# Two-stage fused kernel on one core: the head mix runs two places behind its premix, with six exponent tiles and a 2 KB ring for GpSimd's transfers

## The chip, the cores and the metric

The kernel runs on one core of a Trainium2 chip. A core has a matrix engine (TensorE; PE in the profile, its weight loads PEld), a vector engine (DVE), an activation engine (ACT), GpSimd (POOL) and a queue that only issues transfers (SP). Each engine takes its own instructions strictly in the order in which the program wrote them, and waits on semaphores where it needs the result of another. The metric is the device time of one execution in microseconds; lower is better. The kernel before takes 1709.07 us, the median of three runs (1707.4 to 1711.44).

## The reference

The inputs are q, k and v of 8 batches, 12 heads, 448 tokens and 64 channels, two 12x12 matrices that mix heads, and two weights of a feed-forward layer of width 2048. All is float32.

```python
def _attn_ref(q, k, v, w_pre, w_post):
    scale = 1.0 / np.sqrt(q.shape[-1])
    scores = scale * np.matmul(q, k.transpose(0, 1, 3, 2))
    scores = np.einsum('bhij,hg->bgij', scores, w_pre)
    scores = scores - np.max(scores, axis=-1, keepdims=True)
    attn = np.exp(scores)
    attn = attn / (np.sum(attn, axis=-1, keepdims=True) + 1e-09)
    attn = np.einsum('bhij,hg->bgij', attn, w_post)
    return np.matmul(attn, v)

def _moe_ref(x, w_in, w_out):      # x: 3584 tokens of 768 channels
    h = x @ w_in
    g = h - np.tanh(h)
    return g @ w_out
```

So the attention mixes the heads twice: once before the softmax (w_pre, "premix") and once after it (w_post, "mix").

## The kernel before, in words

The program has an attention part (until about 855 us) and a feed-forward part after it. The change touches the attention part, and through one number the transfers that GpSimd issues in the feed-forward part.

**Blocks and groups.** A block is 120 query tokens of one batch (the fourth of a batch has 88). For each block `scores` (L874) multiplies q and k head by head into PSUM, and ACT and DVE copy the result into the tile `s`, whose rows are tokens (L879). A premix needs the 12 heads of a token on the partitions, so SP gathers 10 tokens x 12 heads = 120 rows of `s` into a tile `t` (`gather`, L907). Such a set of rows is a group; there are 45 groups in a batch and 360 in all. There are six `t` tiles, used in turn.

**Places.** The loop from L1256 on runs over places. Place `p` handles the groups 2p and 2p+1, so there are 180 places (`NPL`), and a few more to run out. At a place the program writes, in this order:

- the copy of the last mix's PSUM into the tile `at` (ACT, L967 or L974), which the loop keeps in the variable `mixed` from the place before;
- a step of `conv`, which turns the feed-forward weights into split parts on ACT, DVE and GpSimd (lines 81 to 131), its transfers being issued by SP (L766);
- the gathers for place p+2;
- `premix(p)`: 4 matmuls with `wpre` into two PSUM tiles `ps_p` (L918). There are only these two, so the next premix needs both exponents of this place done;
- `norm(p-1)`: DVE adds 1e-9 to the row sums `zs` of place p-1 and inverts them (L938, L939), GpSimd multiplies them into the mixing matrix, giving `wr` (L940);
- `expo(p)`: for each of the two PSUM tiles DVE takes the row maximum `mx` (L927) and ACT the exponent `e` with the row sum (L929). There are four `e` tiles, two for each of two places;
- what the planner has put at this place: `scores`, `values`, and the transposes of q (`prep_q`, L840) and of k (`prep_k`, L814);
- `mix(p-1)`: 16 matmuls with `e` as weights and `wr` as the moving side into `ps_o` (L957). There is one `ps_o`, so a mix also needs the `at` copy of the one before.

A matmul on float32 stands as two in the trace, so that a premix has 8 there and a mix 32.

**Values and the planner.** `values(i, t)` multiplies `at` of block i with v for half of the heads (L999). The planner (a list `halved` of jobs with a first and a last place) spreads `scores` and `values` over the places. A values job of block i may begin two places after place (f1-1)//2, in which the last group of the block stands, and is due a place after the place in which the second next block begins. The v tiles `vr` of a batch are loaded by three transfers (from L766's queue; three tiles, so that a load must wait for the values jobs that read the batch before).

**SP's order.** SP issues the gathers, the loads of q, k and v and the transfers of `conv`, all in the order of the places. If one of them waits, those behind it wait too.

**Tail.** At place 180 the loop splits the first token tiles for the feed-forward part, with five casts on ACT (L279), and mixes place 179; block 0 of the feed-forward part (L291 to L294) follows.

In the feed-forward part GpSimd issues 72 transfers of `ga`, `gb` and `gs` tiles (L647, L669, L670), 8 of `go` and 48 stores of the result (L519). The constructor of the program sets aside 4096 bytes per partition for the ring in which GpSimd writes the descriptors of its transfers.

Of the kernel before, what the change touches and what calls it, by code (L numbers as in the profile page):

```python
# [10 lines left out]
F32 = mybir.dt.float32  # L11
# [139 lines left out]
def kernel_body(  # L151
# [11 lines left out]
    nc = tc.nc  # L163
    B, H, S, D = q.shape
    P = 128
# [570 lines left out]
    with ExitStack() as st:  # L736
# [8 lines left out]
        gp = st.enter_context(tc.tile_pool(name="gp", bufs=4, side="right"))  # L745
# [175 lines left out]
        def expo(p, pss):  # L921
            zs = gp.tile([P, 3, 2], F32, name="zs", tag="zs")
            es = []
            for r, ps in enumerate(pss):

                mx = gp.tile([P, 1], F32, name="mx", tag="mx")
                nc.vector.tensor_reduce(out=mx, in_=ps, axis=AX.X, op=ALU.max, negate=True)  # L927
                e = gp.tile([P, S], F32, name="e", tag="e", bufs=4)
                nc.scalar.activation(e, ps, AF.Exp, bias=mx, scale=1.0, accum_out=zs[:, 0, r : r + 1])  # L929
                es.append(e)  # L930
            te[p] = [es, zs]
# [149 lines left out]
        for w in range(2):  # L1081
            for at in AT[w]:
                x = repeat[:, w, at : at + HP].rearrange("p (i h) -> p i h", i=GH)
# [52 lines left out]
        NG = len(groups)  # L1136
# [4 lines left out]
        NPL = NG // 2  # L1141
# [12 lines left out]
        for i in range(len(blocks)):  # L1154

            f0, f1, f2 = first[i : i + 3]
            if i + 1 < len(blocks):
                lo = max(0, (f0 - 1) // 2 - 1)
                hi = f1 // 2 - 3
                for x in range(0 if i else 1, 3):  # L1160
                    e = lo + 2 * x if lo + 4 <= hi else lo + (hi - lo) * x // 2
                    halved.append((e if i else x - 1, hi, "s", i + 1, x))
            for x in range(2):
                halved.append(((f1 - 1) // 2 + 2, f2 // 2 + 1 if f2 < NG else NPL + 7, "v", i, x))
        at_s, p, kind = {}, 0, None
        window = {i: (lo, hi) for lo, hi, k, i, _ in sorted(halved, reverse=True) if k == "s"}
        while halved:
# [84 lines left out]
            NPL - 1: [partial(load_w0, 1)],  # L1252
            NPL + 1: [block0.step],
        }
        mixed = None
        for p in range(NPL + 3):  # L1256
            if mixed:
                mixed()
                mixed = None
            if 5 <= p < NPL + 1:  # L1260
                conv.place()
            place[0] += 1
            for t in (2 * p + 4, 2 * p + 5):
                if t < NG:
                    gather(t)
            issue(6)
            if p == NPL + 1:
                for f in start.pop(p):
                    f()
            if p < NPL:  # L1270
                ps = premix(p)
            if 1 <= p < NPL + 1:
                norm(p - 1)
            if p == NPL:
                for f in x0[1:]:
                    f()
            if p < NPL:
                expo(p, ps)
            if p == NPL + 2:
                next(xq)  # L1280
                next(xq)
            for f, *a in todo[p]:
                f(*a)
            for f in sooner:
                f()
            sooner.clear()
            if 1 <= p < NPL + 1:
                mixed = mix(p - 1)
            for f in then + last:
                f()  # L1290
            then.clear()
            last.clear()
            if p == NPL - 3:
                conv.rest(now)
                early.close()
                open_early()
            if p == NPL - 1:
                early_ps.close()
                open_ps_h()
            for f in start.get(p, ()):  # L1300
                f()
            for _ in range(pieces.get(p, 0)):
                next(xl)
# [91 lines left out]
```

## Time and profile before

| | |
|---|---|
| median of three runs | 1709.07 us (1707.4 to 1711.44) |
| profiled execution, its own time | 1717.03 us |
| span of its profile, first to last instruction | 1715.3 us |
| granted TensorE clock, mean | 0.990 |
| PE busy | 1666.7 us (97%) |
| DVE, ACT, POOL busy | 1233.9 us (72%), 1091.9 us (64%), 586.7 us (34%) |
| premix, mix: busy on PE | 183.1 us, 316.9 us |

The profiled execution is 8.0 us longer than the median of the plain runs. Rows of the profile are read like this: a group of instructions has its line, engine, operation and tiles, the number of instructions, busy time and the mean length of one, and behind the bar the idle time of its engine just before them with what ended it. A row of the table of waits has the waiting engine and tile, who ended the wait, the sum in us, the number of waits and the longest. A row of the timeline has start, length, engine, line and tiles, and in brackets the idle time before it.

### The profile page before, as it was taken

What the parts mean: (1) busy time and instruction counts of PE and PEld (TensorE: products, weight loads), DVE (VectorE), ACT (ScalarE), POOL (GpSimd) and SP (SyncE); (2) the same over time, 40 slices, a digit from 0 to 9 for tenths busy, and PEclk for the clock granted to TensorE, in tenths of its full rate; (3) what the DMA queues carried; (4) which work ended last, traced back from release to release, by engine and by line L of the source; (5) the groups of instructions that cost most, each with busy time, mean ns of one, the idle gap of its engine ahead of it and who ended that gap; (6) DMA issues with size and microseconds to landing.
All of it is one profiled execution on the core that took longest, in us unless ns stands there. A gap on an engine that the chain in (4) does not pass through costs nothing.

```text
span 1715.3 us, 41215 instructions
## 1 busy us (share of the span) xinstructions
PE 1666.7 (97%) x16068; PEld 1385.2 (81%) x16068; DVE 1233.9 (72%) x2119; ACT 1091.9 (64%) x1920; POOL 586.7 (34%) x798
## 2 busy tenths in 40 slices
PE   8999999999999999999999999999999999999999
PEld 6777677777777677677787888888888888889999
DVE  5777767868767677775478899858888868778432
ACT  5776777767667677776577677565667455665331
POOL 1566667767657666663100011101001101101100
PEclk9999999999999999999999999999999999999999
DMA  8779879887878878866579799988999989988993
GB/s 184 217 228 257 255 232 277 250 255 247 242 236 247 256 229 260 263 190 210 193 255 339 259 325 311 342 306 322 318 341 354 368 267 339 317 311 326 400 414 136
DMA packets 322290, 475.09 MB, mean 277 GB/s; under 512 B 105264, under 2 KB 255280, under 8 KB 322096
## 3 DMA queue, kind: packets, MB, share of 16 engines
q1 hardware_dynamic: 305660, 414.34, 74.7%
q0 software_dynamic: 16128, 57.68, 8.7%
q8 instruction: 128, 2.10, 0.5%
q14 instruction: 66, 0.54, 0.1%
q10 hardware_dynamic: 308, 0.43, 0.1%
HBM read 274.73 MB, written 120.59 MB: 230 GB/s over the span
## 4 chain that ended last, share of the span: by engine, by line
PE 70%; DMA 10%; DVE 7%; ACT 5%; issue 4%; POOL 3%; SPq 1%; ACTq 0%; POOLq 0%; DVEq 0%
PE ps_o L957 11%; PE ps_h L291 7%; PE ps_h L292 7%; PE ps_h L294 7%; PE ps_m L999 6%; PE ps_p L918 6%; PE y L534 6%; PE y L532 5%; PE y L533 5%; PE ps_q L874 4%; DMA t<-s 3%; DMA gl<-gs 2%; ACT e L929 2%; DMA vr<-in_v_dram 1%; DMA w<-wo 1%
## 5 line engine op out<-in xcount | busy, mean ns | idle before, releaser
L957 PEld LDWEIGHTS ps_o<-wr,e 60*112 60x112 f32 (+1 forms) x5760 | 306.0, 176 | 45.5 <-POOL wr L940 31.3
L957 PE MATMUL ps_o<-wr,e 60*112 60x60 f32 (+1 forms) x5760 | 316.9, 260 | 15.8 <-POOL wr L940 14.5
L929 ACT ACTIVATE e<-ps_p,mx 128x448 f32<-128x448 f32 x360 | 225.1, 632 | 119.1 <-DVE mx L927 88.4
L927 DVE TENSOR_REDUCE mx<-ps_p 128x1 f32<-128x448 f32 x360 | 206.7, 616 | 112.8 <-PE ps_p L918 112.3
L967 ACT COPY at<-ps_o 112x960 f32<-112x960 f32 x156 | 154.5, 990 | 110.6 <-PE ps_o L957 110.2
L918 PE MATMUL ps_p<-t,wpre 60*64 60x448 f32 (+1 forms) x1440 | 183.1, 572 | 8.5 <-DMA t<-s 7.1
L999 PEld LDWEIGHTS ps_m<-at,vr 112*64 112x64 f32 x3072 | 149.8, 138 | 25.7 <-ACT at L974 7.5
L999 PE MATMUL ps_m<-at,vr 112*64 112x120 f32 (+1 forms) x3072 | 164.1, 264 | 3.2 <-DMA vr<-in_v_dram 2.9
L532 PE MATMUL y<-w,gh 128*128 128x384 f32 x448 | 151.2, 337 | 3.6 <-DMA w<-wo 2.2
L940 POOL TENSOR_TENSOR wr<-wpost,zs 128x120 f32<-128x120 f32 x180 | 70.1, 390 | 243.0 <-DVE zs L939 198.4
L533 PE MATMUL y<-w,gh 128*128 128x384 f32 x448 | 150.3, 336 | 0.0
L534 PE MATMUL y<-w,gl 128*128 128x384 f32 x424 | 143.3, 338 | 2.6 <-DVE gl L450 2.5
L874 PEld LDWEIGHTS ps_q<-kk,qh 64*120 64x120 f32 (+1 forms) x768 | 59.5, 175 | 82.9 <-issue 45.8
L874 PE MATMUL ps_q<-kk,qh 64*120 64x448 f32 (+1 forms) x768 | 122.6, 396 | 1.2 <-DVE kk L826 0.5
L879 DVE COPY s<-ps_q 120x448 f32<-120x448 f32 (+1 forms) x192 | 112.4, 615 | 8.3 <-PE ps_q L874 8.1
L669 POOL DMA_DIRECT2D gs<-gb x24 | 17.3, 720 | 295.4 <-DVE gb L668 295.4
L307 ACT ACTIVATE u<-h 128x1024 f32<-128x1024 f32 x56 | 59.5, 1063 | 75.0 <-DVE h L716 70.8
L879 ACT COPY s<-ps_q 120x448 f32<-120x448 f32 (+1 forms) x192 | 95.1, 539 | 7.0 <-PE ps_q L874 6.7
L647 POOL DMA_DIRECT2D gs<-ga x24 | 17.2, 719 | 229.5 <-DVE ga L330 229.5
L532 PEld LDWEIGHTS y<-w,gh 128*128 128x128 f32 x448 | 84.2, 188 | 8.8 <-issue 2.8
L533 PEld LDWEIGHTS y<-w,gh 128*128 128x128 f32 x448 | 84.1, 188 | 3.4
L534 PEld LDWEIGHTS y<-w,gl 128*128 128x128 f32 x424 | 79.5, 188 | 4.2 <-DVE gl L450 4.2
(372 smaller groups left out, 3974.1 us busy)
## 6 DMA issues: line engine op xcount, KB each, us to landing
t<-s SPq DMA_DIRECT2D x342, 210.0 KB
wa<-ss SPq DMA_DIRECT2D x96, 384.0 KB
w<-wo SPq DMA_DIRECT2D x43, 768.0 KB
gl<-gs SPq DMA_DIRECT2D x62, 512.0 KB
wa<-wi SPq DMA_DIRECT2D x72, 384.0 KB
w<-ts SPq DMA_DIRECT2D x35, 768.0 KB
gs<-gs POOLq DMA_DIRECT2D x24, 768.0 KB, 9.0
cr<-in_moe_w_in_dram SPq DMA_DIRECT2D x48, 256.0 KB
```

The costliest lines, as they stand in the source:

```text
L291: nc.tensor.matmul(ph, w[:, c, 0], xh, start=start and c == 0, stop=False, skip_group_check=True)
L532: nc.tensor.matmul(y, gh[:, tok], wh, start=first, stop=False, skip_group_check=True)
L533: nc.tensor.matmul(y, gh[:, tok], wl, start=False, stop=False, skip_group_check=True)
L534: nc.tensor.matmul(y, gl[:, tok], wh, start=False, stop=last, skip_group_check=True)
L874: nc.tensor.matmul(ps[:n, :S], qx[a, hp, :], kx[a, hp % 2], start=(x == 0), stop=(x == 2))
L879: eng(sts[i][:n, 2 * hp + j, :], ps[:n, :S])
L918: nc.tensor.matmul(pss[r][halves[j], :], wpre[k, :], ts[j][k, :], start=True, stop=True)
L927: nc.vector.tensor_reduce(out=mx, in_=ps, axis=AX.X, op=ALU.max, negate=True)
L929: nc.scalar.activation(e, ps, AF.Exp, bias=mx, scale=1.0, accum_out=zs[:, 0, r : r + 1])
L957: nc.tensor.matmul(ps[:CP, j, c * GP : (c + 1) * GP].rearrange("p (h i) -> p h i", i=GI)[:, :, r * GH : (r + 1) * GH], e[k, c * CP : (c + ...
L967: nc.scalar.copy(ats[i0][:, :, :, at : at + 2 * GI].rearrange("p c h (j i) -> p j (c h) i", j=2), ps[:CP, :, : NC * GP].rearrange("p j (x ...
L999: nc.tensor.matmul(pv[j * D : (j + 1) * D, r, :n], vt[:, j, c, :], ats[i][:, c, 2 * hp + j, :n], start=(c == 0), stop=(c == NC - 1),)
```

## The change

The loop keeps the mix one place longer: at place p it now writes `mix(p-2)` where it wrote `mix(p-1)`. `norm(p-1)` stays where it was, so `wr` of a mix is written one place ahead of it. At place 180 the mixes of places 178 and 179 both stand, with the `at` copy of 178 between them. For this the `e` tiles become six, and the ring of GpSimd's transfers shrinks from 4096 to 2048 bytes per partition; the two additional `e` tiles take 3584 bytes. The values jobs begin and are due a place later.

```diff
-                e = gp.tile([P, S], F32, name="e", tag="e", bufs=4)
+                e = gp.tile([P, S], F32, name="e", tag="e", bufs=6)
...
-                halved.append(((f1 - 1) // 2 + 2, f2 // 2 + 1 if f2 < NG else NPL + 7, "v", i, x))
+                halved.append(((f1 - 1) // 2 + 3, f2 // 2 + 2, "v", i, x) if f2 < NG else ((f1 - 1) // 2 + (3 if f1 < NG else 2), NPL + 7, "v", i, x))
...
-        mixed = None
+        mixed = []
         for p in range(NPL + 3):
-            if mixed:
-                mixed()
-                mixed = None
+            for f in mixed:
+                f()
+            mixed.clear()
...
-            if 1 <= p < NPL + 1:
-                mixed = mix(p - 1)
+            if 2 <= p < NPL + 1:
+                mixed.append(mix(p - 2))
+            if p == NPL:
+                mixed.pop()()
+                mixed.append(mix(p - 1))
...
-    nc = _bacc.Bacc("TRN2", target_bir_lowering=False, num_devices=1, dynamic_dma_scratch_size=4096)
+    nc = _bacc.Bacc("TRN2", target_bir_lowering=False, num_devices=1, dynamic_dma_scratch_size=2048)
```

What this moves, at three places of the program. First TensorE at places 0 to 3; a row has the line, what is written and read, the size and the number. Before:

```order
L918 MATMUL ps_p<-t,wpre 64x448 x4
L874 MATMUL ps_q<-kk,qh 120x448 x4
L874 MATMUL ps_q<-kk,ql 120x448 x2
L957 MATMUL ps_o<-wr,e 112x12x5 x16
L918 MATMUL ps_p<-t,wpre 64x448 x4
L874 MATMUL ps_q<-kk,qh 120x448 x4
L874 MATMUL ps_q<-kk,ql 120x448 x2
L957 MATMUL ps_o<-wr,e 112x12x5 x16
```

These rows begin with the premix of place 1, and the first mix stands behind the scores of that place. With the change, from the same premix on:

```order
L918 MATMUL ps_p<-t,wpre 64x448 x4
L874 MATMUL ps_q<-kk,qh 120x448 x4
L874 MATMUL ps_q<-kk,ql 120x448 x2
L918 MATMUL ps_p<-t,wpre 64x448 x4
L874 MATMUL ps_q<-kk,qh 120x448 x4
L874 MATMUL ps_q<-kk,ql 120x448 x2
L957 MATMUL ps_o<-wr,e 112x12x5 x16
```

Place 1 has no mix any more, and from there on each mix stands one premix and one set of scores later; GpSimd's order has not changed anywhere.

Second, SP around the three loads of v of the second batch, with what each transfer waits for (DMAHW: an earlier transfer; PE, DVE, Pool: an engine). Before:

```order
L766 DMA vr<-in_v_dram 112x4x256 [waits DMAHW3_49]
L766 DMA xs_57<-x 768x1x208 [waits DMAHW4_49,DVE_49]
L766 DMA cr<-in_moe_w_in_dram 128x2x256 [waits DMAHW5_49,Pool_49]
L766 DMA cr<-in_moe_w_in_dram 128x2x256 [waits DMAHW6_49]
L907 DMA t<-s 120x1x448 [waits DMAHW7_49,PE_49]
L907 DMA t<-s 120x1x448 [waits DMAHW0_49]
L766 DMA qr<-in_q_dram 88x12x64 [waits DMAHW1_49]
L766 DMA vr<-in_v_dram 112x4x256 [waits DMAHW2_49]
```

None of the loads of v waited for an engine here. With the change:

```order
L766 DMA vr<-in_v_dram 112x4x256 [waits DMAHW3_49,PE_49]
L766 DMA cr<-in_moe_w_in_dram 128x2x256 [waits DMAHW4_49,Pool_49]
L766 DMA cr<-in_moe_w_in_dram 128x2x256 [waits DMAHW5_49]
L907 DMA t<-s 120x1x448 [waits DMAHW6_49,PE_49]
L907 DMA t<-s 120x1x448 [waits DMAHW7_49]
L766 DMA qr<-in_q_dram 88x12x64 [waits DMAHW0_49]
L766 DMA vr<-in_v_dram 112x4x256 [waits DMAHW1_49,PE_49]
L766 DMA wi_66<-co 512x1x256 [waits DMAHW2_49,Pool_49]
L907 DMA t<-s 120x1x448 [waits DMAHW3_49]
```

The loads now carry a wait for TensorE, since the values jobs that read the old v tiles stand two places later; the same holds for the third of these loads and for the batches with index 3, 5 and 7. In the batches 2, 4 and 6 only the second load waits for TensorE, and it did so before.

Third, ACT at the tail, places 178 to 180. Before:

```order
L279 CAST xh<-xl 128x512
L967 COPY at<-ps_o 112x2x48x10
L929 ACTIVATE e,zs<-ps_p,mx 128x448 x2
L967 COPY at<-ps_o 112x2x48x10
L279 CAST xh<-xl 128x512 x5
L974 COPY at<-ps_o 112x48x9 x2
```

The five casts stood ahead of the last `at` copy, which no mix waits for. With the change:

```order
L279 CAST xh<-xl 128x512
L967 COPY at<-ps_o 112x2x48x10
L929 ACTIVATE e,zs<-ps_p,mx 128x448 x2
L967 COPY at<-ps_o 112x2x48x10
L279 CAST xh<-xl 128x512 x5
L967 COPY at<-ps_o 112x2x48x10
L974 COPY at<-ps_o 112x48x9 x2
```

One more `at` copy, that of place 178, now stands behind the casts, and the mix of place 179 needs it.

## The prediction

> **What bounds the kernel now.** I read the windows first. Columns: time, then busy us of PE, PEld, DVE, ACT and POOL with their instructions, granted clock, DMA share, GB/s.
>
> ```profile
> 25.00:855.00 830.00, 803.86 (x11629) 615.68 (x11630) 595.49 (x1506) 582.90 (x1335) 495.48 (x641) 0.98 0.79 238
> 855.00:1715.30 860.30, 842.65 (x4296) 753.34 (x4296) 627.18 (x589) 499.17 (x567) 84.41 (x130) 1.00 0.88 317
> ```
>
> TensorE sets the pace in both parts; in the attention part it is idle for 830.0 - 803.9 = 26.1 us. The table of waits says what ends its idle time there (sum, number, longest):
>
> ```profile
> PEld ps_o L957 <- POOL wr L940: 31.3, 43, 2.1
> PE ps_o L957 <- POOL wr L940: 14.5, 17, 1.7
> PE ps_p L918 <- DMA t<-s: 7.1, 6, 1.8
> PE ps_m L999 <- DMA vr<-in_v_dram: 2.9, 2, 1.9
> ```
>
> So the largest wait is the one of the mix for `wr`, in 43 of 180 places at its weight load, and in 17 long enough to be seen at the matmul. Next I looked at such places in the timeline. In this one POOL is late:
>
> ```profile
> 727.34 0.37 PE L874 MATMUL ps_q<-kk,ql 64*120 64x448 f32 x2
> 727.72 0.62 ACT L929 ACTIVATE e<-ps_p,mx 128x448 f32<-128x448 f32 x1
> 728.73 0.55 POOL L940 TENSOR_TENSOR wr<-wpost,zs 128x120 f32<-128x120 f32 x1
> 729.33 1.78 PE L957 MATMUL ps_o<-wr,e 60*112 60x60 f32 x32 [1.62 <-POOL wr L940]
> ```
>
> The scores end at 727.71, `wr` comes behind other work of POOL, and TensorE stands for 1.62 us; the exponent of this place has long ended, at 728.34. In the next one DVE is late, and everything with it:
>
> ```profile
> 100.39 0.98 PE L918 MATMUL ps_p<-t,wpre 60*64 60x448 f32 x8
> 101.81 0.37 PE L874 MATMUL ps_q<-kk,ql 64*120 64x448 f32 x2
> 102.41 0.43 DVE L94 TENSOR_SCALAR co<-cr 128x512 int32<-128x512 int32 x1
> 103.08 1.14 DVE L927 TENSOR_REDUCE mx<-ps_p 128x1 f32<-128x448 f32 x2
> 103.75 1.78 PE L957 MATMUL ps_o<-wr,e 60*112 60x60 f32 x32 [1.57 <-POOL wr L940]
> 104.40 0.62 ACT L929 ACTIVATE e<-ps_p,mx 128x448 f32<-128x448 f32 x1
> 105.46 0.98 PE L918 MATMUL ps_p<-t,wpre 60*64 60x448 f32 x8
> ```
>
> DVE works for `conv` (L94), so both the row sums that `wr` needs and the maxima that this place's exponents need come late. The next premix needs the second exponent, which ends at 105.02.
>
> **The change, term by term**, against the profiled execution (span 1715.3, own time 1717.0 us).
>
> *The wait for `wr`.* The mix of place p-2 needs a `wr` that was due one place earlier, so this wait goes. What it costs now lies between 14.5 us (idle at the matmuls) and 31.3 us (idle at the weight loads). A weight load that waits lets the matmul before it run out first:
>
> ```profile
> L957 PE MATMUL ps_o<-wr,e 60*112 60x60 f32 (+1 forms) x5760 | 316.9, 260 | 15.8 <-POOL wr L940 14.5
> ```
>
> With 0.26 us for one matmul, 31.3 - 43 x 0.26 = 20.1. I take -20.
>
> *The pace of a mix behind a wait.* A mix that had waited takes 105.46 - 103.75 = 1.71 us from its start to the premix; one that had not:
>
> ```profile
> 401.46 1.70 PE L957 MATMUL ps_o<-wr,e 60*112 60x60 f32 x32
> 403.09 0.98 PE L918 MATMUL ps_p<-t,wpre 60*64 60x448 f32 x8
> ```
>
> That is 1.63. 43 x 0.08 = 3.4, at least nothing: I take -3.
>
> *The clock.* Behind some waits the granted clock is halved:
>
> ```profile
> 211.06 1.78 PE L957 MATMUL ps_o<-wr,e 60*112 60x60 f32 x32 [1.57 <-POOL wr L940]
> 212.90:216.30 3.40, 3.40 (x18) 1.77 (x20) 2.84 (x7) 2.05 (x5) 3.24 (x5) 0.50 0.80 284
> 471.18 1.04 PE L999 MATMUL ps_m<-at,vr 112*64 112x120 f32 x16 [1.89 <-DMA vr<-in_v_dram]
> 472.40:479.00 6.60, 6.60 (x52) 4.83 (x52) 3.35 (x9) 2.71 (x6) 1.67 (x2) 0.50 0.91 302
> ```
>
> Half of 3.4 and half of 6.6 us are 1.7 + 3.3 = 5.0 lost. The wait of 1.57 us at 103.75 above has no such stretch behind it, so it is partly luck: I take -3 (0 to -5). The Trainium skill ("TensorE: Matmul & The Clock Gate", Part 1) gives such a window as about 3.4 us and lets the clock fall only after a whole idle one; by that rule this term would be 0 and the sum 3 us higher. The trace disagrees in that waits of 1.57 and 1.89 us are followed by it.
>
> *Loads of v.* In the plan of the change the values jobs that need a new v tile stand a place or two later, so that the 2.9 us of waiting for `vr` (the one at 471.18 is most of it) should go: -2 (0 to -2.9).
>
> *The exponents.* With no wait at the mix, TensorE comes to the next premix earlier and waits there for the exponents instead, where DVE is late. At 100.39: scores end 102.18, a mix of 1.63 ends 103.81, the exponent 105.02: 1.2 of the 1.57 us come back. At 727.34: 727.71 + 1.63 = 729.34 is behind 728.34, so nothing comes back. I did this sum for all 17 waits. In 6 the exponent is later, from the one at 103.75 (1.2) to this last one:
>
> ```profile
> 573.40 0.37 PE L874 MATMUL ps_q<-kk,ql 64*120 64x448 f32 x2
> 575.03 1.78 PE L957 MATMUL ps_o<-wr,e 60*112 60x60 f32 x32 [1.26 <-POOL wr L940]
> 575.69 0.62 ACT L929 ACTIVATE e<-ps_p,mx 128x448 f32<-128x448 f32 x1
> ```
>
> (573.77 + 1.63 = 575.40 against 576.31: 0.9.) Together they make about 4.5, between 0 and the whole 20: +4.5.
>
> *The gathers.* The chain of waits has gathers of this length from issue to landing (start, length), and a wait for one stands just behind the wait for `wr` at 575.03:
>
> ```profile
> 176.46 7.13 DMA t<-s
> 583.03 0.98 PE L918 MATMUL ps_p<-t,wpre 60*64 60x448 f32 x8 [0.86 <-DMA t<-s]
> ```
>
> TensorE waits 7.1 us for gathers already. In such a place it now only comes to the gather sooner, if SP does not follow. I take half of those 7.1 us once more, +3.5, between 0 and 20.
>
> *The tail.* At place 180 two mixes stand with one PSUM tile between them:
>
> ```profile
> 848.62 1.78 PE L957 MATMUL ps_o<-wr,e 60*112 60x60 f32 x32 [0.26 <-ACT at L967]
> 850.44 0.98 ACT L967 COPY at<-ps_o 112x960 f32<-112x960 f32 x1
> 851.31 2.69 ACT L279 CAST xh<-xl 128x512 fp32r<-128x512 f32 x5
> 851.56 3.25 PE L957 MATMUL ps_o<-wr,e 60*112 60x60 f32 x32 [1.16 <-POOL wr L940]
> ```
>
> Now: 0.26 + 1.16 = 1.4 us of waiting. With the change the mix of 178 waits for one copy (about 1.2 with its start), and that of 179 for five casts and a copy, 2.69 + 0.98 = 3.7, less the 1.7 of the mix between: 2.0. 1.2 + 2.0 - 1.4 = +1.8 (1 to 3.5). Place 1 merely does without its mix: 0.
>
> *The ring.* In the feed-forward part POOL has 84.4 of 860.3 us of work. Its transfers come like this:
>
> ```profile
> 1213.16 0.73 POOL L669 DMA_DIRECT2D gs<-gb  x1 [13.06 <-DVE gb L668]
> 1223.13 0.72 POOL L647 DMA_DIRECT2D gs<-ga  x1 [8.50 <-DVE ga L330]
> gs<-gs POOLq DMA_DIRECT2D x24, 768.0 KB, 9.0
> gs<-ga POOLq DMA_DIRECT2D x24, 512.0 KB, 5.7
> gs<-gb POOLq DMA_DIRECT2D x24, 512.0 KB, 6.5
> ```
>
> Even if the smaller ring let each start only when the one before has landed, the three would take 9.0 + 5.7 + 6.5 = 21.2 us, and they come once in 13.06 + 8.50 and some 2 us of issuing, about 23.8. So 0, covered by POOL's idle time; if the cover were gone, DVE's next write of `gb` would be late by the difference, 24 times. The Trainium skill ("DMA: Bandwidth & Descriptors", Terms and The descriptor swizzle) has descriptors of 16 bytes and 9 of them per engine and side for 1 MiB, by which 2 KB would hold 128, an estimate, and the 1.25 MiB of `gb` and `gs` together some 11; no row here can show it.
>
> The sum: -20 - 3 - 3 - 2 + 4.5 + 3.5 + 1.8 = -18.2. The median of the plain runs is 8.0 us below the profiled one, and if part of that is fewer such stalls, there is a little less to win: I take -16, so 1709.07 - 16 = 1693 us.
>
> **Rivals.**
>
> *The gathers decide (nothing gained).* If SP is the pace and not TensorE, the 20 + 3 us only move from the mix to the premix, and with the tail the time is 1709 + 1.8 - 2 = 1709. For it: DMA share 0.79 over the attention part and gathers waited for today. Against: only 6 waits of 180.
>
> *Part of it.* Exponents and gathers take back 20 rather than 8, because DVE (595.5 of 830 us busy) and the DMA engines (0.79) are late more often behind a quicker TensorE: 1709 - 18.2 + 12 = 1703. For it: the place at 100.39, where most of the wait comes back. Against: in 11 of the 17 waits nothing did.
>
> *SP is held by the loads of v (slower).* In four batches all three loads of v now carry a wait for TensorE. A load that stands in the place of its values job waits for that place's premix (0.98 us above) and values, and the gathers behind it wait too:
>
> ```profile
> 837.81 2.68 PE L999 MATMUL ps_m<-at,vr 112*64 112x120 f32 x48
> 463.08 0.42 SPq L766 DMA_DIRECT2D vr<-in_v_dram  x1
> ```
>
> 0.98 + 2.68 = 3.7 us for each of 12 loads is 44 us. It outweighs the gain from 18 / 12 = 1.5 us for each on; at 2 us, 24 - 18 = +6: 1715 us. For it: the order of the program. Against: in the even batches a load with that wait (the one at 463.08) is issued in 0.42 us, and of three loads only the second stands in the place of its job; with 4 x 3.7 = 15 us it would not quite cancel the gain, and the gathers, issued two places ahead, cover some of that.
>
> **How the numbers follow.** Forecast 1693, its own range 1685 to 1702: 0.64. Part of it (1702 to 1705.5): 0.13. Nothing gained (1706 to 1712): 0.12. SP held (from 1712 on): 0.11. About 0.2% (3.4 us) is what a measurement of this kernel can tell from no change. Faster 0.77, same 0.12, slower 0.11. With every saving at its bound (31.3 + 3 + 5 + 2.9) and the costs as taken (9.8) it would be 1709 - 32 = 1677; I leave out the last part of that. Range 1683 to 1710.
>
> **What would show it.** In the profile after: no row "ps_o L957 <- POOL wr"; a row "ps_p L918 <- ACT e" of some 4 to 5 us; "ps_p L918 <- DMA t<-s" of 7 to 11 us; no long wait for vr; fewer stretches at half clock; two waits for `at` of 1 to 2 us at the tail; the feed-forward part at 860 us as before. It is wrong if the waits for t grow past 20 us, if SP's loads of v take over 1.5 us each, or if POOL's transfers take more than their 0.73 us to issue and the feed-forward part becomes longer.

## The result: the change is slower by 0.8%

Median 1723.7 us (1720.8 to 1730.4, 11 runs) beside 1709.3 us for the kernel before (1703.2 to 1723.3, 11 runs): ratio 1.0076, 95% interval [1.0056, 1.0097]. The forecast was 1693 us, its range 1683 to 1710: wrong in sign. The profiled execution of the change took 1720.8 us (span 1719.1), that of before 1717.0 us (span 1715.3); so the spans of the two profiles differ by 3.8 us where the medians differ by 14.4: as the prediction had noted, before's profiled execution lies some 8 us above its median.

The windows of the change (time, busy us of PE, PEld, DVE, ACT, POOL with their instructions, granted clock, DMA share, GB/s):

```profile
25.00:855.00 830.00, 805.46 (x11596) 622.02 (x11596) 596.00 (x1506) 581.24 (x1335) 496.06 (x640) 0.98 0.80 239
855.00:1719.10 864.10, 846.70 (x4328) 757.28 (x4328) 626.91 (x589) 499.45 (x568) 84.47 (x131) 0.99 0.88 316
```

TensorE is idle for 24.5 us of the attention part (before 26.1) and for 17.4 us of the rest (before 17.7). The second window begins at a fixed time and so holds the end of the attention part too; from the end of the last mix to the end of the span the two kernels take the same, 860.5 us before and 860.4 us now. The loss is no idle time at first sight. The table of waits of the change:

```profile
PE ps_p L918 <- DMA t<-s: 16.3, 12, 3.2
PE ps_p L918 <- ACT e L929: 5.6, 8, 1.1
PE ps_o L957 <- ACT at L967: 2.6, 3, 1.2
PEld ps_p L918 <- ACT e L929: 15.7, 32, 1.2
```

The row of `wr` at the matmuls is gone (at the weight loads three waits of 3.0 us in all are left), and so is that of `vr`. In their place stand the gathers (7.1 us before) and the exponents. The exponents show only in part as waits of a matmul: the page's groups have the premix itself longer. Of the kernel before, then of the change:

```profile
L918 PE MATMUL ps_p<-t,wpre 60*64 60x448 f32 (+1 forms) x1440 | 183.1, 572 | 8.5 <-DMA t<-s 7.1
```

```profile
L918 PE MATMUL ps_p<-t,wpre 60*64 60x448 f32 (+1 forms) x1440 | 193.3, 570 | 23.1 <-DMA t<-s 16.3
```

10.2 us more of "busy" for the same 1440 matmuls. A premix writes two PSUM tiles, each of which is free when an exponent of the place before has read it. The first exponent lets the premix begin; until the second has ended it stands in its middle, and the profile counts that as work. From the starts of the eight matmuls of each premix: 33 of 180 are stretched by more than 0.1 us, 13.7 us in all; before it was 7, and 2.5 us. One such place in the timeline of the change:

```profile
682.34 0.69 DVE L91 SCALAR_TENSOR_TENSOR cr<-cm,co 128x512 int32<-128x512 int32 x1
683.06 0.71 DVE L94 TENSOR_SCALAR co<-cr 128x512 int32<-128x512 int32 x1
684.01 1.13 DVE L927 TENSOR_REDUCE mx<-ps_p 128x1 f32<-128x448 f32 x2
684.71 0.63 ACT L929 ACTIVATE e<-ps_p,mx 128x448 f32<-128x448 f32 x1 [2.05 <-DVE mx L927]
685.34 0.62 ACT L929 ACTIVATE e<-ps_p,mx 128x448 f32<-128x448 f32 x1
685.49 1.59 PE L918 MATMUL ps_p<-t,wpre 60*64 60x448 f32 x8 [1.10 <-ACT e L929]
686.10 0.20 PEld L918 LDWEIGHTS ps_p<-t,wpre 64*64 64x64 f32 x6 [0.43 <-ACT e L929]
```

DVE works for `conv` until 683.77, the maxima and with them the exponents are late, and the premix waits 1.10 us at its start and then takes 1.59 us where 0.98 is its length: 0.61 us more, which no row of waits of the matmuls has.

Stretches at half clock, with the wait that each stands behind (timeline, then windows, of the change; the second stretch begins inside its wait):

```profile
158.88 1.05 PE L918 MATMUL ps_p<-t,wpre 60*64 60x448 f32 x8 [2.36 <-DMA t<-s]
478.08 1.77 PE L918 MATMUL ps_p<-t,wpre 60*64 60x448 f32 x8 [3.19 <-DMA t<-s]
```

```profile
159.70:163.10 3.40, 3.40 (x28) 2.92 (x24) 2.36 (x5) 2.29 (x6) 3.32 (x3) 0.50 1.00 293
477.10:483.90 6.80, 5.82 (x44) 4.26 (x46) 1.93 (x4) 1.90 (x6) 2.73 (x3) 0.50 0.84 219
```

Inside the span such stretches are 41.0 us (before 34.7), so about 3.2 us more are lost to them in these two profiles. More is to be had from all runs: the span of each times its mean granted clock is the time that it would have taken at full clock, the rest is lost to the clock. Medians: before 1694.3 us at full clock and 14 to 17 lost, the change 1698.7 and 22.4. So some 4 us of the loss are there at full clock, and 5 to 9 us more are lost to the clock.

### The profile page after: what moved, and what is told of

It reads as the page before. It is cut to its first block, busy times and chain, and to the rows that moved or that the text cites. A ratio compares the mean times of both kernels' runs of the same rounds, so it can differ in the third digit from the quotient of the medians.

```text
span 1719.1 us, 41201 instructions
## 1 busy us (share of the span) xinstructions
PE 1673.1 (97%) x16068; PEld 1396.1 (81%) x16068; DVE 1234.2 (72%) x2119; ACT 1090.5 (63%) x1920; POOL 587.3 (34%) x798
## 4 chain that ended last, share of the span: by engine, by line
PE 81%; DMA 9%; DVE 4%; ACT 3%; issue 2%; POOL 1%; SPq 1%; ACTq 0%; DVEq 0%; POOLq 0%
PE ps_o L957 13%; PE ps_p L918 8%; PE ps_m L999 8%; PE ps_h L291 8%; PE ps_h L292 8%; PE ps_h L294 7%; PE ps_q L874 6%; PE y L532 6%; PE y L534 6%; PE y L533 6%; DMA t<-s 4%; DMA w<-wo 2%; DMA gl<-gs 1%; PE ps_m L840 1%; PE y L504 1%
## 5 line engine op out<-in xcount | busy, mean ns | idle before, releaser
L957 PEld LDWEIGHTS ps_o<-wr,e 60*112 60x112 f32 (+1 forms) x5760 | 309.0, 176 | 20.8 <-issue 6.0
L957 PE MATMUL ps_o<-wr,e 60*112 60x60 f32 (+1 forms) x5760 | 313.6, 259 | 2.6 <-ACT at L967 2.6
L918 PE MATMUL ps_p<-t,wpre 60*64 60x448 f32 (+1 forms) x1440 | 193.3, 570 | 23.1 <-DMA t<-s 16.3
```

The source lines that it names most:

```text
L918: nc.tensor.matmul(pss[r][halves[j], :], wpre[k, :], ts[j][k, :], start=True, stop=True)
L957: nc.tensor.matmul(ps[:CP, j, c * GP : (c + 1) * GP].rearrange("p (h i) -> p h i", i=GI)[:, :, r * GH : (r + 1) * GH], e[k, c * CP : (c + ...
```

## The experiments

Three theories stood behind the first runs. **Late DVE**: `wr` and the exponents wait for the same late engine, so a wait that is removed at the mix comes back at the premix. **Gathers held on SP**: loads of v and transfers of `conv` that wait for an engine hold the gathers behind them. **The plan**: placing the values jobs one place later costs time by itself. A fourth, **alignment**, was formed later.

**One part of the change at a time.** The ring alone:

```diff
-dynamic_dma_scratch_size=4096
+dynamic_dma_scratch_size=2048
```

> The kernel before with the 2 KB ring alone, nothing else of the change. Ring theory (the smaller ring slows the feed-forward part): 1716 to 1724 us, and the stretch behind the attention part longer than 860 us. All the others (exponents, SP, clock): the same as before, 1709 us within 4, POOL's transfers at 0.72 to 0.76 us each.

Measured 1713.1 us, ratio 1.0015 [0.9992, 1.0037]: no difference that can be told.

The later values alone, with the mix still one place behind:

```diff
-halved.append(((f1 - 1) // 2 + 2, f2 // 2 + 1 if f2 < NG else NPL + 7, "v", i, x))
+halved.append(((f1 - 1) // 2 + 3, f2 // 2 + 2, "v", i, x) if f2 < NG else ...
```

> The kernel before with the later values jobs alone; the mix stays one place behind. SP theory (loads of v wait for TensorE and hold the gathers): most of the loss is here, 1716 to 1722 us, and the waits for t in the attention part 12 us or more instead of 7. Exponent theory (the lost cover of the mix's wait): the same as before, 1709 us within 4, the waits for wr still 14 us at the matmul.

Measured 1739.8 us, ratio 1.0161 [1.0132, 1.0190]. Its waits:

```profile
PE ps_o L957 <- POOL wr L940: 22.5, 31, 2.2
PE ps_p L918 <- DMA t<-s: 12.9, 8, 2.6
```

Both theories had expected 1722 us at most. So, with `conv` where it stands, the later values cost 30 us while the mix is one place behind, and the deeper mix takes 16 of them back. That these are the 16 us of the forecast is a coincidence: they start from 22.5 us of waits for `wr` and not from 14.5. Of the 30 us about half is there at full clock (1709.0 beside 1694.8), the rest is the clock.

**SP, DVE's order, the mixture of places.** Loads of v one place later, in the change:

```diff
-at_place(p0 + 4 + hq, load_v, b, hq)
+at_place(p0 + 5 + hq, load_v, b, hq)
```

> The changed kernel, with each load of v put one place later, so that in the odd batches two of three loads no longer wait for TensorE. SP theory: the waits for t fall from 16 to 9 us and the time to 1712 to 1718 us. Exponent theory: 1723 us within 4, and the row of the premix waiting for the exponent stays at 5 to 6 us.

Measured 1719.5 us, ratio 1.0048 [1.0028, 1.0068] to the kernel before: 4 us less than the change, at the edge of what can be told (quotient of the two ratios 0.997 [0.994, 1.000]). The waits for t fell from 16.3 to 13.8 us. SP's own waits show the hold: at these loads SP waits for the matmuls of values 8.5 us in the change (four waits of up to 2.8 us), and not at all in the kernel before or with this edit. So the hold is there, and it is a small part of the loss.

`conv` behind the maxima and exponents of each place, in the change and in the kernel before:

```diff
-            if 5 <= p < NPL + 1:
-                conv.place()
 ...
                 expo(p, ps)
+            if 5 <= p < NPL + 1:
+                conv.place()
```

> The changed kernel, with the step of conv written behind the exponents instead of ahead of the premix, so that DVE takes the maxima before conv's instructions. Exponent theory: the premix waits for the exponent in few places (under 2 us in the row, and hardly any premix stretched inside) and the time falls by 8 to 15 us to 1708 to 1715. SP theory: no gain, 1720 to 1728 us, since SP then waits for conv's transfers even later.

> The kernel before with conv placed behind the exponents' maxima of each place. Theory 'late DVE': the row sums and the maxima come before conv's work on DVE, so the wait for wr falls from 14.5 to under 6, but the copies of the scores come behind conv, so the gathers are later as in the change with the same edit (t 7 to 15): median 1704 to 1712. Theory 'SP': conv's transfers are issued as before, the waits for t stay at 7, and what wr loses is won: 1696 to 1702.

Measured 1733.2 us in the change (ratio 1.0118 [1.0092, 1.0144]) and 1730.0 us in the kernel before (1.0117 [1.0088, 1.0145]), both above every range that had been expected. In the change the exponents wait less (2.6 us for 5.6) and the gathers more:

```profile
PE ps_p L918 <- DMA t<-s: 20.8, 13, 3.8
PE ps_o L957 <- ACT at L967: 3.4, 6, 1.2
PE ps_p L918 <- ACT e L929: 2.6, 6, 0.7
```

In the kernel before with this edit `wr` falls from 14.5 to 10.2 us and t rises from 7.1 to 12.3. Either order of DVE's work makes something late, and the one that both kernels have is the better.

`norm` behind the exponents, in the change:

```diff
-            if 1 <= p < NPL + 1:
-                norm(p - 1)
 ...
                 expo(p, ps)
+            if 1 <= p < NPL + 1:
+                norm(p - 1)
```

> The change with the row sums' reciprocals (norm) behind the maxima and exponents of the place; wr has a place of slack now, so nothing waits for it. Three small DVE operations, 0.4 to 0.6 us, go from ahead of the maxima to behind them. Theory 'the hidden exponents took the gain': the second exponent ends about 0.5 us sooner, the time inside the premixes falls from 13 to under 6 and the waits for e from 5.6 to under 3, 6 to 10 us less, median 1714 to 1718. Theory 'gathers decide': the exponents fall alike but the gathers take it, 1720 to 1725.

Measured 1728.4 us, ratio 1.0115 [1.0088, 1.0141]: the exponents wait longer, not shorter.

```profile
PE ps_p L918 <- ACT e L929: 8.6, 12, 1.5
PEld ps_p L918 <- ACT e L929: 20.5, 40, 1.6
```

```profile
L82 DVE TENSOR_SCALAR cr<-cr 128x512 int32<-128x512 int32 x48 | 58.7, 1224 | 0.0
```

This expectation was wrong in its arithmetic. As I read it, which no run tests, `norm` runs on DVE while TensorE is in the premix, when the maxima could not start in any case; behind the exponents it takes time from the copies of the scores. The last row (DVE's groups) shows a second cost: the same 48 steps of `conv` take 58.7 us, where they take 39.0 in the kernel before and 44.5 in the change (see the last section).

`conv`'s transfers issued by GpSimd in place of SP, in the change:

```diff
-                    send(x, nc.sync)
+                    send(x, nc.sync if x is queue else nc.gpsimd)
```

> The change with the transfers of conv issued by GpSimd and not by SP, so that SP no longer stands before a transfer that waits for conv's engines while a gather is behind it. Theory 'gathers held on SP': the waits for t fall from 16.3 to under 8, with them the half-clock stretches, 8 to 12 us less, median 1711 to 1716. Theory 'late DVE' (the waits only move between wr, exponents and gathers): t falls and the exponents take it, under 4 us less, 1720 to 1725. Rival: some 192 issues at about 0.7 us each are 140 us more for POOL in 830, conv and wr come later, slower: over 1728.

Measured 1765.3 us, ratio 1.0332 [1.0301, 1.0362]: the rival. POOL's work in the attention part rises from 496 to 635 us (the window), and the waits for t and for the exponents double, so that this run does not tell what SP's waits for `conv` cost:

```profile
25.00:855.00 830.00, 784.22 (x10908) 600.48 (x10910) 605.61 (x1440) 551.39 (x1271) 634.58 (x817) 0.96 0.76 228
```

```profile
PE ps_p L918 <- DMA t<-s: 34.5, 15, 5.1
PE ps_p L918 <- ACT e L929: 11.5, 14, 2.6
```

The mixture of places: with the later values the transposes of k fall into places with values (17 of 21, before 11), and more places hold one score job alone (44, before 42). Half of that undone:

```diff
-                o = max(p + 4, o + 1)
+                o = max(p + 5, o + 1)
```

> The change with the transposes of k one place later (p + 5 in place of p + 4), which makes the mixture of places stand halfway back: k with values 14 places (before 11, change 17), k with one score job 7 (before 10, change 4), places with one score job in all 44 as in the change. Theory 'the mixture of the plan costs it': half of what the mixture costs comes back; the later values alone cost 30 us with the mix one place behind and the change 14, so 5 to 10 us come back, median 1714 to 1719, fewer us of exponents inside the premixes (13 now). Theory 'gathers held on SP': the loads and the queue are as before, median 1721 to 1726, waits for t 14 to 19.

Measured 1726.3 us, ratio 1.0099 [1.0076, 1.0122]: no gain where the theory had expected 5 to 10 us. This one trial speaks against the mixture as such.

Gathers three places ahead, with eight tiles (and the 2 KB ring), in the kernel before:

```diff
-        RT = 6
+        RT = 8
 ...
-            for t in (2 * p + 4, 2 * p + 5):
-                if t < NG:
-                    gather(t)
+            while sent_t[0] < min(2 * p + 8, NG) and (sent_t[0] < 2 * p + 6 or end_s.get((groups[sent_t[0]][0], 2), -1) < p):
+                gather(sent_t[0])
+                sent_t[0] += 1
```

> A trial of another version: the kernel before with the 2 KB ring and eight tiles for gathers in place of six, each gather issued three places ahead where its scores are done, else two. In the profile of before 7.1 us are waits for gathers, with half-clock stretches behind some of them. Theory 'gathers': t falls to under 2 us, half of the 13.7 us lost at half clock goes, 8 to 14 us faster, 1696 to 1702. Theory 'the waits only move': t falls but wr takes it, within 3 us of before. Rival: the bursts of gathers at the batch boundaries hold conv's and q's loads on SP, slower.

Measured 1729.7 us, ratio 1.0104 [1.0075, 1.0133]: slower. The gathers are hardly waited for any more, and the loads of v are in their place; that the bursts of gathers ahead of them on SP hold them is my reading:

```profile
PE ps_o L957 <- POOL wr L940: 16.9, 21, 1.7
PE ps_m L999 <- DMA vr<-in_v_dram: 13.2, 7, 3.3
PE ps_p L918 <- DMA t<-s: 1.6, 1, 1.6
```

**`conv` taken out of the places.** By now every edit had moved waits about. Both kernels without `conv`'s steps in the attention part, all of them done in one go at place 177:

```diff
-            if 5 <= p < NPL + 1:
+            if NPL <= p < NPL + 1:
                 conv.place()
```

> The kernel before with none of conv's work in the places 5 to 176: all of it is done in one go at place 177, which makes the whole longer by an unknown time (some 100 to 300 us); what counts is the time at which the places up to 176 are done, and the waits in them. Theory 'late DVE by conv': the wait for wr falls from 14.5 us at the matmuls to under 3, the waits for t to under 3, no half-clock stretch in the attention part. Theory 'the plan itself': wr falls by less than half.

> The same edit on the changed kernel, to be set beside the one on the kernel before. Theory 'late DVE by conv, the waits only move': the exponents in the premixes and the waits for t fall under 3 us, and the places up to 176 take the same as in the kernel before with the edit, within 3 us; whole time 0 to 6 us above it. Theory 'the plan itself' (later values cost 30, the deeper mix gives 16 back): the places still take 10 us or more longer. Theory 'depth helps, but conv takes it back': the places take 5 us or more less than in the kernel before with the edit.

Measured 2153.2 us for the kernel before with the edit and 2152.8 for the change with it (ratios to the kernel before 1.2581 [1.2554, 1.2608] and 1.2578 [1.2551, 1.2605]). The windows up to place 175 and, from the timeline, the premix of place 176; of the kernel before with the edit, then of the change with it:

```profile
25.00:790.00 765.00, 763.09 (x11326) 594.20 (x11327) 443.58 (x1238) 517.17 (x1184) 67.71 (x175) 1.00 0.52 153
```

```profile
790.86 1.43 PE L918 MATMUL ps_p<-t,wpre 60*64 60x448 f32 x8
```

```profile
25.00:790.00 765.00, 762.17 (x11308) 593.62 (x11308) 444.13 (x1239) 517.10 (x1186) 67.73 (x175) 1.00 0.52 154
```

```profile
790.04 1.21 PE L918 MATMUL ps_p<-t,wpre 60*64 60x448 f32 x8
```

TensorE is idle for 1.9 and 2.8 us of 765, the clock is full. In the profiles with `conv` in the places that premix begins at 833.28 (before) and 833.46 (change): in these two profiles meeting `conv` costs some 43 us in either kernel. At this premix the change has one mix of 1.63 us less behind it, so at equal work it is 0.8 us later without `conv`, and 1.8 us with it. Without `conv` the plan with later values costs nothing that can be told, and the deeper mix, with nothing to wait for, gains nothing. The theory "the plan itself" falls: the later values cost time only together with `conv`. That it matters which of `conv`'s steps meet which places is what the next runs test.

**Alignment.** `conv` takes a step of its jobs in each place, so starting it one or two places later moves its steps on DVE, POOL and ACT by as much against the plan:

```diff
-            if 5 <= p < NPL + 1:
+            if 6 <= p < NPL + 1:
```

and `7 <= p` likewise.

> The change with conv started at place 6 and not 5: the same work in the same plan, but each of its steps on DVE falls one place later, so that they meet other kinds of places (behind a place with one score job 26 of its 88 steps, 21 now; behind values without k 23, 27 now). Theory 'phase' (the time depends on which places conv's DVE steps meet): the exponents and gathers wait 5 us or more longer, 1729 to 1740. Theory 'plan and depth': within 3 us of the change, 1720.7 to 1726.7.

> The kernel before with conv started at place 6 and not 5. Theory 'alignment': the kernel before stands better than its neighbours, so this one is 4 to 15 us slower, 1714 to 1726, more waits for wr than 14.5. Theory 'the change costs it in every alignment': within 4 us of before, 1706 to 1714.

> The kernel before with conv started at place 7. Theory 'alignment': 4 to 15 us slower than before, 1714 to 1726. Theory 'the change costs it in every alignment': 1706 to 1714.

> The change with conv started at place 7 (start at 5: 1723.7, at 6: 1716.7). Theory 'alignment': anywhere from 1708 to 1726, and the mean over the three starts is no more than that of the kernel before over its three. Theory 'the change costs it in every alignment': 1715 or more, the mean over three starts 8 us or more above that of the kernel before.

An alignment that is no shift, the 48 jobs spread over ten more places:

```diff
-        conv = Convert(nc, cv, partial(dma, to=slow), quads, NPL - 24)
+        conv = Convert(nc, cv, partial(dma, to=slow), quads, NPL - 14)
```

> The kernel before with conv's 48 jobs spread over 166 places and not 156 (NPL - 14 for NPL - 24), so that its steps fall on other places and come 6% more rarely. Theory 'alignment': the kernel before loses its alignment, 1718 to 1738, waits for wr over 18. Theory 'the rate counts more': 1700 to 1712.

> The same edit on the change. Theory 'alignment': 5 to 20 us below the kernel before with the edit, 1712 to 1726. Theory 'the change costs it in every alignment': 5 us or more above the kernel before with the edit. As a version: under 1706 it would beat both.

Medians and ratios to the kernel as it was before; the last column is the quotient of the two ratios, its interval from their half widths added in squares:

| `conv` | kernel before, us | with the deeper mix, us | change / before |
|---|---|---|---|
| from place 5 (as it is) | 1709.3 | 1723.7, 1.0076 | 1.0076 [1.0056, 1.0097] |
| from place 6 | 1729.6, 1.0113 [1.0084, 1.0143] | 1716.7, 1.0028 [1.0011, 1.0044] | 0.992 [0.988, 0.995] |
| from place 7 | 1738.3, 1.0144 [1.0113, 1.0175] | 1727.2, 1.0084 [1.0062, 1.0105] | 0.994 [0.990, 0.998] |
| spread | 1732.5, 1.0115 [1.0089, 1.0142] | 1715.6, 1.0021 [1.0003, 1.0038] | 0.991 [0.988, 0.994] |
| all at place 177 | 2153.2 | 2152.8 | 1.000 [0.997, 1.003] |

In three alignments of four the deeper mix is the faster by 11 to 17 us. Only where `conv` starts at place 5 is it slower: there the kernel before stands 17 to 26 us below its own other alignments (each beside the kernel before of the same rounds), more than the 4 to 15 us that I had expected for the starts at 6 and 7, while the change moves within 12 us over its four. My expectation for the start at place 6 in the change was a miss: from the order of DVE's instructions alone I had taken it for a worse alignment, and it was 7 us better.

The profiles of these runs say what stays and what moves (us; in each column the kernel before with the edit, then the change with it):

| `conv` | premix of place 176 begins | waits for `wr` at the matmuls | premixes, busy | waits for t |
|---|---|---|---|---|
| from place 5 (as it is) | 833.3, 833.5 | 14.5, 0 | 183.1, 193.3 | 7.1, 16.3 |
| from place 6 | 848.0, 828.1 | 22.5, 0 | 184.4, 194.7 | 3.7, 13.9 |
| from place 7 | 854.7, 840.9 | 25.6, 0 | 185.4, 194.6 | 5.7, 20.2 |
| spread | 847.2, 831.7 | 26.2, 0 | 185.5, 192.0 | 3.2, 19.7 |

The premixes of the second row, in the kernel before and in the change, both with `conv` from place 6:

```profile
L918 PE MATMUL ps_p<-t,wpre 60*64 60x448 f32 (+1 forms) x1440 | 184.4, 578 | 7.2 <-DMA t<-s 3.7
```

```profile
L918 PE MATMUL ps_p<-t,wpre 64*64 64x448 f32 (+1 forms) x1440 | 194.7, 570 | 20.6 <-DMA t<-s 13.9
```

With the deeper mix the premixes are 6.5 to 10.3 us longer, and the gathers are waited for 9 to 17 us more, in every alignment. These costs belong to the deeper mix beside `conv`, and not to one alignment of the two. What the alignment changes is mostly the other side: how long the kernel before waits for `wr`, and so how much there is to save.

What the alignment does, in one place. In the kernel before, as it is, two DVE steps of `conv` (L81, L82) stand ahead of place 130, which has transposes of k besides its one score job:

```profile
627.64 1.52 DVE L82 TENSOR_SCALAR cr<-cr 128x512 int32<-128x512 int32 x1
628.89 0.99 PE L814 MATMUL ps_m<-ident,kr 112*128 112x112 f32 x8
630.26 0.39 POOL L940 TENSOR_TENSOR wr<-wpost,zs 128x120 f32<-128x120 f32 x1
630.31 0.37 PE L874 MATMUL ps_q<-kk,ql 64*120 64x448 f32 x2
630.70 1.78 PE L957 MATMUL ps_o<-wr,e 60*112 60x60 f32 x32
```

`wr` ends at 630.65, the scores at 630.68: nobody waits. With `conv` one place later the same two steps meet place 131, a score job and nothing else, and DVE comes to them late from the copies of k:

```profile
641.42 1.16 DVE L826 TENSOR_TENSOR kk<-ps_m,kk 128x448 fp32r<-128x448 f32 x2 [0.36 <-ACT kk L825]
642.88 1.52 DVE L82 TENSOR_SCALAR cr<-cr 128x512 int32<-128x512 int32 x1
643.37 0.37 PE L874 MATMUL ps_q<-kk,ql 64*120 64x448 f32 x2
644.86 0.39 POOL L940 TENSOR_TENSOR wr<-wpost,zs 128x120 f32<-128x120 f32 x1 [0.75 <-DVE zs L939]
645.31 1.78 PE L957 MATMUL ps_o<-wr,e 60*112 60x60 f32 x32 [1.57 <-POOL wr L940]
```

The scores end at 643.74, `wr` at 645.25, and the mix waits 1.57 us. I counted, in each trace, the places with one score job and no values in which DVE works 1.5 us or more for `conv`, a step belonging to the premix behind whose start it begins. With the mix one place behind: 6 in the kernel before (wait for `wr` 14.5 us), 9 with `conv` spread (26.2), 12 from place 6 (22.5), 13 from place 7 (25.6), 13 with the later values (22.5). The kernel before has the fewest and the least wait. With the deeper mix the count (16, 12, 6 and 7 for the starts at 5, 6, 7 and spread) does not order the times. The count also hangs on how it is made: by the overlap in time, the kernel before as it is and with `conv` spread have 4 such places each. It was chosen after the runs, so it is an account of the difference and not a tested rule.

The clock has its part. At full clock the change takes 1698.7, 1696.5, 1698.9 and 1692.6 us in the four rows, and loses 22.4, 18.0, 26.8 and 21.5 to the clock; the kernel before takes 1694.3, 1705.3, 1705.9 and 1695.2, and loses 14 to 17, 22.5, 29.5 and 35.5. With `conv` spread nearly the whole difference between the kernels is the clock.

**The two best edits of the change together**, `conv` from place 6 and the loads of v one place later:

> The change with conv started at place 6 (alone 7 us less) and the loads of v one place later (alone 4 us less). If the two add, 1712 to 1714, level with before or 2 to 3 us above it. If they touch the same gathers at the batch boundaries, 1716 to 1718. Theory 'alignment' has no sum rule: 1708 to 1724.

Measured 1717.9 us, ratio 1.0025 [1.0006, 1.0044]: the two do not add. No version that was run beats the kernel before; the nearest, the deeper mix with `conv` spread, is 0.2% behind it.

## Why the prediction was wrong, by its own steps

| term | predicted, us | the two profiles, us |
|---|---|---|
| the wait for `wr` | -20 | -20 (still the estimate: 14.5 gone at the matmuls, 28.3 at the weight loads) |
| pace of a mix behind a wait | -3 | -3.3 (L957 busy 316.9, now 313.6) |
| loads of v | -2 | -2.9 (row gone) |
| exponents | +4.5 | +15.8 (5.6 of waits, 10.2 inside the premixes) |
| gathers | +3.5 | +9.2 (7.1, now 16.3) |
| tail | +1.8 | +0.9 (1.17 + 1.16, less 1.4) |
| clock | -3 | +3.2 (half of 41.0 less 34.7) |
| ring | 0 | 0 |
| sum | -18.2 | +2.9, against +3.8 between the spans |

The first three terms and the ring fit the forecast, the first of them within wide bounds. The waits of the tail came out smaller than forecast:

```profile
848.77 1.78 PE L957 MATMUL ps_o<-wr,e 60*112 60x60 f32 x32
851.73 2.52 PE L957 MATMUL ps_o<-wr,e 60*112 60x60 f32 x32 [1.17 <-ACT at L967]
855.40 3.25 PE L957 MATMUL ps_o<-wr,e 60*112 60x60 f32 x32 [1.16 <-ACT at L967]
```

The term of the tail had left out the clock: from 852.6 to 862.8 us stands a stretch of 10.2 us at half clock, where the kernel before has 6.8 us. All four alignments of the change have 10.2 us there, those of the kernel before 3.4 or 6.8. In the table its 1.7 us are part of the row of the clock.

**The step that failed first is the one on the loads of v**: it read the later values jobs as a gain of 2 us and put no price on what else moves: 42 of the 64 values jobs stand one or two places later, 39 of the 184 score jobs one place earlier or later, 22 of the 42 transposes of k one or two places earlier, each against `conv`. Alone they cost 30 us with `conv` where it stands, and nothing that can be told without it. No term of the sum had `conv` in it beyond the places where TensorE already waited, and it is `conv` that sets nearly all waits of this part (without it TensorE is idle for 1.9 and 2.8 us of 765).

**The exponents were mis-sized, 4.5 for 15.8.** The sum went over the 17 places where a wait for `wr` stood in the old profile. The new waits stand in 33 premixes, and they are no accident of one alignment: the traces of the change have 29 to 34 such premixes in all four, those of the kernel before 2 to 7. And I looked for them as a row of waits ("4 to 5 us", it is 5.6) where two thirds are inside the premix.

**The gathers, 3.5 for 9.2**, are of the same kind, 9 to 17 us in the four alignments. The later values alone already raise the waits for t from 7.1 to 12.9 us. With the gathers goes **the clock, -3 for +3.2**. The waits for gathers are fewer and longer than those for `wr` (12 of up to 3.2 us beside 17 of up to 1.7), and seven of the eight half-clock stretches that begin between 25 and 855 us in the change start in or behind one of them. By the rule of the Trainium skill quoted in the prediction ("TensorE: Matmul & The Clock Gate", Part 1) the clock term would be 0; it was +3.2 in the two profiles and 5 to 9 in the medians.

**The rivals.** "Part of it", exponents and gathers taking back 20 in place of 8, is what happened in kind: 25 in place of 8. "The gathers decide" put the whole on SP, which the runs with earlier gathers and with later loads do not bear out. "SP is held by the loads of v" was on the right side by luck: its mechanism shows as 8.5 us of SP's time where the rival had 15 to 44, and taking it away gains some 4 us of the 14. The rival that was missing: the kernel before stands in an alignment with its other work that an edit to its order may lose. Each of the six edits to that order that kept `conv` in the places cost it 1.0 to 1.6%; whether it was tuned to stand so or stands so by luck, no run here tells.

Of the signs named, those of `wr`, `vr`, the tail and the feed-forward part showed right; "t 7 to 11 us" and "fewer stretches at half clock" showed it wrong. None of the three signs that were to tell of a failure came: t waited 16.3 us and not over 20, 3 of SP's 24 loads of v took over 1.5 us (before 4), and POOL's transfers took 0.71 us as before. They watched SP and POOL, and the costs stood elsewhere.

Open: where all of the 14.4 us stand, since no profile holds them. The run with the ring alone, the kernel before in all but that, has a profile nearer to the median (span 1711.1 us); the change's is 8.0 us longer, of which 4.7 us stand at the end of the last mix and 3.2 us behind it. Also open: why the deeper mix has its own spread of 12 us over the alignments, which the count of places does not order; and why the premixes of an alignment wait for gathers in clusters that halve the clock, which was seen and not taken apart.

## What to carry to other kernels

When an edit moves jobs in a plan that shares its engines with a second stream of work, price the move against that stream, or at least measure both versions in several alignments of the two (shift the stream by a place): here the verdict went from 0.8% slower to 0.6 to 0.9% faster. A wait for PSUM inside a group of matmuls does not show as a wait of the matmuls; compare the busy time of the same instructions before and after, and read the weight loads' waits. A wait removed at one instruction is won only if the engine that was late is late for nothing else.

## What the runs showed of the hardware

**A step of DVE takes longer where POOL works.** The step L82 of `conv`, the same instruction 48 times, takes 0.42 us where POOL does nothing by the profile's spans (30 of 48 times in the kernel before), and on average 1.47 us where POOL works through it (18 times; in the change 22 of 48 stand free, 26 under POOL, on average 1.36 us). Its groups, of the kernel before and of the change:

```profile
L82 DVE TENSOR_SCALAR cr<-cr 128x512 int32<-128x512 int32 x48 | 39.0, 813 | 0.0
```

```profile
L82 DVE TENSOR_SCALAR cr<-cr 128x512 int32<-128x512 int32 x48 | 44.5, 927 | 0.0
```

So an alignment also sets how long a step of `conv` is, and the two steps L82 in the places shown above are of the long kind. The lengths alone do not order the times: in the kernel before with `conv` spread 40 of the 48 stand free, and it takes 1732.5 us. The Trainium skill ("SBUF — State Buffer", Who interferes with whom) has it that a `tensor_scalar` on DVE can run in a mode in which it needs the pair of ports that it shares with GpSimd, and that whichever of the two issues first then has the pair for its whole instruction while the other is blocked. The two lengths on DVE, 0.42 and 1.47 us, agree with that; whether POOL's operations are held as well stays open.

**Most of the spread between runs is the clock.** In the five sets of 11 to 23 runs of the kernel before that the experiments were compared with, the spans have a standard deviation of 3.3 to 3.8 us, the spans times their mean granted clock one of 1.5 to 2.7, and the time lost to the clock goes with the span (correlation 0.82 to 0.92). Half-clock stretches of 3.4 us, or a multiple of it, stand behind waits of 1.4 to 3.2 us, sometimes behind shorter ones, and not behind every one. In each trace of the kernels of the two tables by alignment their starts lie whole multiples of 3.413 us apart (39, 100, 102, 132 and so on of them behind the first in the change), so they begin on a fixed grid of times and not at the waits themselves.
